# Attention scores of two chunks at a time, with four masks in 32-row tiles and eight PSUM banks

## The chip, the cores and the metric

The kernel runs on one core of one Trainium2 chip. The core has TensorE (matmuls; its weight loads are shown apart as PEld), VectorE (DVE), ScalarE (ACT), GpSimd (POOL) and SyncE (SP, which issues nearly all DMAs here). Matmul results go to PSUM, eight banks of 128 partitions by 512 float32. Everything else lies in SBUF, here one buffer called `arena`. The metric is the device time of one execution in microseconds (us).

## The reference

Routed attention, then an MLP mixer:

```python
q_assign = argmax(einsum('bhsd,hcd->bhsc', q_n, c_n), -1)   # 16 clusters per head
k_assign = argmax(einsum('bhsd,hcd->bhsc', k_n, c_n), -1)
mask   = q_assign[:, :, :, None] == k_assign[:, :, None, :]
scores = where(mask, q @ k.T / sqrt(64), -1e9)
attn   = softmax(scores);  x = attn @ v                     # B 4, H 8, S 768, D 64
h = relu(x.transpose(0, 2, 1) @ w_tok1) @ w_tok2            # 768 -> 256 -> 768
u = x + h.transpose(0, 2, 1)
out = u + relu(u @ w_ch1) @ w_ch2                           # 512 -> 1536 -> 512
```

All is float32. The change touches the attention alone.

## The kernel before, in words

The 32 heads are worked off as 16 pairs (`pair(m)`). In a pair head 0 has partitions 0 to 63 and head 1 partitions 64 to 127 of the transposed q and k, `Ts[m % 3]`, so that the two heads of one step go to TensorE as two row tiles of 64 rows, at positions (0, 0) and (64, 0), with results in two PSUM banks.

`scores(m)` works in twelve chunks: six blocks of 128 keys (`i`) by two halves of 384 queries (`u`). For each chunk and head there is one float32 matmul of 64 rows (`plain`; each float32 matmul becomes two instructions on TensorE), and onto the same bank one bf16 matmul, the mask: key one-hots times query one-hots of the clusters, scaled so that pairs of different clusters get about -2**33. The one-hots are in `Ms[m % 2]`, rows 64h to 64h + 16; the rows up to the tile's end are zero. After that ScalarE takes the exp of both banks (L1205) into the `exs` buffers. Three pairs of banks are used in turn (`s = n % 3`, banks 0 to 5); banks 6 and 7 belong to the values. Pair 0 is built a little otherwise: its first three chunks' scores run ahead of the masks.

After the scores come the values (`values`, L1238): for each of the six key blocks sixteen matmuls in 128 by 32 tiles, four side by side, added up in banks 6 and 7. After the first of them stand the sums of the pair before (`sums(m - 1, 5)`), which are softmax denominators: a matmul of ones with `es`, the exps added up by DVE. `add_up` makes two half sums `es[0]` and `es[1]` with four additions of 128x1536; where `FOLD[m]` is "V", DVE adds these two together as well and `sums` needs one group of matmuls, where it is "-" it needs two. Before the fifth block stands `route(m + 2, 0)`: four matmuls with the centroids into bank 0, on DVE a transpose (L1098), a maximum (L1099), a comparison and a transpose (L1103), on ScalarE a scaling to bf16 (L1108). That result goes to DRAM (`wdm`) and back into `Ms` with two DMAs, one for each head. `finish_x` has DVE transpose the values out of banks 6 and 7 (L1285), transpose the sums (L1293), and, every second pair, divide.

ScalarE also splits q and k of a later pair into 16-bit halves for a DMA transpose (`part_qk`) and joins the halves (`join_qk`), both at L875, eight copies in a pair. DVE meanwhile rounds the mixer's weights piece by piece and stores combinations of them for later.

The order of the work is fixed in the program. TensorE runs in the order of the code. For the other engines a planner (`Program.plan`) simulates the kernel with costs written in the code (`COST`, the numbers at `mm`, `SWITCH = 0.1` where a matmul's tile shape, `mode`, differs from that of the one before) and picks at each time the ready operation with the earliest due time. On the chip each engine keeps that order, and semaphores do the waiting.

After the attention come token mixing and channel mixing, in which TensorE works with 128 by 128 tiles and DVE and POOL combine operands and results. These parts are not edited, but their order on DVE, ACT, POOL and SP comes from the same plan.

Of the kernel before, what the change touches and what calls it, by code (L numbers as in the profile page):

```python
# [19 lines left out]
C = 16  # L20
P = 128
NJ = S // P
# [7 lines left out]
HJ = NJ // 2  # L30
HS = HJ * P
# [18 lines left out]
GRAIN = 32  # L50
BUSY, HITS_AT = 12, 18.0
CHECK_AT = 532.0
FOLD = "-VVVVVVVVVV-----"

COST = {
    "ACT": (0.09, 0.00083),
# [667 lines left out]
def kernel(  # L724
# [26 lines left out]
    nc = tc.nc  # L751
    g = Program()
# [9 lines left out]
    wdm = [dram.tile([P, HS], BF16, name=f"wdm{i}") for i in range(2)]  # L762
# [77 lines left out]
    def bank(*i):  # L840
        return [("ps", n) for n in i]


    def mm(dst, lhsT, rhs, start, stop, cost, rd, wr, pos=None, tr=None):
        def fn(e):
            nc.tensor.matmul(  # L846
                dst, lhsT=lhsT, rhs=rhs, start=start, stop=stop, tile_position=pos,
                is_transpose=tr, skip_group_check=True,
            )

        return g.add({"PE": cost}, fn, rd, wr, mode=(lhsT.shape[0], lhsT.shape[1]))

    def turn(dst, src, rd, wr, start=True, stop=True):
        return mm(
# [46 lines left out]
    def dma(dst, src, rd, wr, kb, row, after=0.0, queue="SP"):  # L901

        q = {"SP": nc.sync, "ACT": nc.scalar, "POOL": nc.gpsimd}[queue]
        return g.add(
            {queue: ISSUE}, lambda e: q.dma_start(dst, src), rd, wr, (kb * 1024, row), after  # L905
        )
# [172 lines left out]
    def route(m, bk):  # L1079

        T, M, hp = Ts[m % 3], Ms[m % 2], m % (H // 2)
        for gr in range(4):
            r0 = (NJ + HJ * gr) % NQK
            mm(
                ps[32 * gr : 32 * gr + 32, bk, 0:HS], cbd.ap[:, hp],
                T.ap[:, r0 : r0 + HJ].rearrange("p a t -> p (a t)"), True, True, 0.161,
                T.rows(r0, r0 + HJ) + cbd.k(), bank(bk), pos=(0, 32 * gr),
            )  # L1090
        a, e, o = rt[0:3]
        if m == 0:
            o = o0

        def blocks(t):
            return t.ap.rearrange("p (n c) -> p n c", c=C)

        vec(lambda: nc.vector.transpose(out=a.ap, in_=ps[:, bk, 0:HS]), 0.57, bank(bk), a.k())  # L1098
        vec(lambda: nc.vector.reduce_max(out=mxs.ap[:, 0:24], in_=blocks(a), axis=AX.X), 0.54,  # L1099
            a.k(), mxs.k())  # L1100
        tt(blocks(e), blocks(a), mxs.ap[:, 0:24].unsqueeze(2).to_broadcast([P, 24, C]),
           ALU.is_ge, HS, a.k() + mxs.k(), e.k())
        vec(lambda: nc.vector.transpose(out=o.ap, in_=e.ap), 0.56, e.k(), o.k())  # L1103

        r = rb if m else rb0
        g.add(
            {"ACT": 0.75},
            lambda e: nc.scalar.activation(  # L1108
                out=r.ap, in_=o.ap, func=ACT.Identity, scale=msc.ap[:, 0:1],
                bias=msc.ap[:, 1:2], accum_out=hits.ap[:, m : m + 1],  # L1110
            ),
            o.k() + msc.k(), r.k() + [("hits", m)], after=0.0 if m else HITS_AT,
        )

        if m == 0:
            for gr in (0, 2, 3, 1):
                i, u = divmod(gr, 2)
                for h in range(2):
                    rows = slice(32 * gr, 32 * gr + 32)
                    dst = M0.ap[64 * h : 64 * h + 32, i, u * HS : (u + 1) * HS]  # L1120

                    def place0(e, dst=dst, rows=rows, i=i, h=h):
                        sc = [msc0.ap[rows, n, h : h + 1] for n in range(2)]
                        if e == "ACT" and i:
                            nc.scalar.activation(
                                out=dst, in_=o.ap[rows], func=ACT.Identity, scale=sc[0], bias=sc[1]
                            )
                        elif e == "ACT":
                            nc.scalar.copy(out=dst, in_=o.ap[rows])  # L1129
                        elif i:  # L1130
                            nc.vector.tensor_scalar(
                                out=dst, in0=o.ap[rows], scalar1=sc[0], scalar2=sc[1],
                                op0=ALU.mult, op1=ALU.add,
                            )
                        else:
                            nc.vector.tensor_copy(out=dst, in_=o.ap[rows])

                    g.add(
                        {"ACT": (0.5, 0.65)[i], "DVE": (0.35, 0.45)[i]}, place0,
                        o.k() + msc0.k() + M0.k(), [("mask", 0, i, u, h)],  # L1140
                    )
            for Mn in Ms:
                vec(
                    lambda Mn=Mn: nc.vector.memset(Mn.ap, 0.0), 0.7,
                    [("mask", 0, 1, u, h) for u in range(2) for h in range(2)], Mn.k(),
                )
            return
        dma(wdm[m % 2], rb.ap, rb.k(), [("wdm", m % 2)], 96, 768)
        for h in range(2):
            dma(  # L1150
                M.ap[64 * h : 64 * h + C].rearrange("c i (u n) -> c (i u) n", u=2),
                wdm[m % 2].rearrange("(g r) n -> r g n", g=4)[C * h : C * h + C],
                [("wdm", m % 2)] + M.k(),
                [("mask", m % 2, i, u, h) for i in range(2) for u in range(2)], 48, 768,
            )


    nex = 0
# [2 lines left out]
    def scores(m):  # L1161
        nonlocal nex
        T, M = Ts[m % 3], Ms[m % 2] if m else M0
        st = unit[m] = [exs[(nex + i) % len(exs)] for i in range(NJ)]
        nex += NJ

        def chunk(n):
            return divmod(n, NJ) if m == 0 else divmod(n, 2)[::-1]

        def plain(n):  # L1170
            u, i = chunk(n)
            s, r0 = n % 3, NJ + HJ * u
            for h in range(2):
                hs = slice(64 * h, 64 * h + 64)
                mm(
                    ps[:, 2 * s + h, 0:HS], T.ap[hs, i],
                    T.ap[hs, r0 : r0 + HJ].rearrange("p a t -> p (a t)"), True, False, 0.3225,
                    T.rows(i, i + 1) + T.rows(r0, r0 + HJ), bank(2 * s + h), pos=(64 * h, 0),
                )

        ahead = 3 if m == 0 else 0
        for n in range(ahead):
            plain(n)
        if m == 0:
            turn_qk(1, (7, 6, 7))
            load_qkr(3, 18.0)
        for n in range(2 * NJ):
            u, i = chunk(n)
            s = n % 3
            if n >= ahead:  # L1190
                plain(n)
            for h in range(2):
                hs = slice(64 * h, 64 * h + 64)
                mm(
                    ps[:, 2 * s + h, 0:HS], M.ap[hs, 1, i * P : (i + 1) * P],
                    M.ap[hs, 0, u * HS : (u + 1) * HS], False, True, 0.081,
                    [("mask", m % 2, a, c, h) for a, c in ((1, i // HJ), (0, u))] + M.k(),
                    bank(2 * s + h), pos=(64 * h, 0),
                )
            if m == 0 and n == ahead - 1:  # L1200
                route(1, 6)
            ex = st[i]
            g.add(
                {"ACT": 0.70},
                lambda e, ex=ex, s=s, u=u: nc.scalar.activation(  # L1205
                    out=ex.ap[:, :, u * HS : (u + 1) * HS], in_=ps[:, 2 * s : 2 * s + 2, 0:HS],
                    func=ACT.Exp, scale=SM_SCALE,
                ),
                bank(2 * s, 2 * s + 1),
                ex.rows(0, 2, u * HS, (u + 1) * HS) + ([("exps", m)] if n == 2 * NJ - 1 else []),  # L1210
            )

    def add_up(m):
        st = unit[m]
# [113 lines left out]
    def pair(m):  # L1328
        scores(m)
        if m >= 1 and m + 2 < NP:  # L1330
            join_qk(m + 2)
        if m:
            next_qk(m)
        for i in range(NJ):
            if i == 3 and m == 0:
                turn_qk(2, (1, 2, 3))
            if i == 4 and 1 <= m < NP - 2:
                route(m + 2, 0)
            if i == 1:
                if m:  # L1340
                    sums(m - 1, 5)
                    finish_x(m - 1, 5, 1)
                add_up(m)
            values(m, i)
        if m == NP - 1:
            sums(m, 4)
        finish_x(m, 5, 0)
        if m == NP - 1:
            finish_x(m, 4, 1)
        if m == 0:  # L1350
            load_v(2)
            route(2, 5)
            next_qk(m)
        if m + 3 < NP:
            load_v(m + 3)
# [620 lines left out]
    for m in range(NP):  # L1976
        pair(m)
# [78 lines left out]
```

## Time and profile before

| | |
|---|---|
| median of 3 runs | 789.91 us (789.84 to 790.67) |
| profiled execution | 789.87 us, its span 788.0 us |
| TensorE busy | 777.8 us, 99% of the span |
| DVE, ACT, POOL busy | 675.2, 461.4, 194.1 us |
| chain that ended last | 95% TensorE |
| granted TensorE clock | 0.999 |
| one pair in steady state | 19.3 us, attention until about 335 us |

The busy shares say how full an engine is over the whole span. The chain of work that ended last is followed back from the last instruction, at each step to what released it. In time order it tells how long TensorE spends on each step of a pair. A matmul row of the trace is longer than the time for which the next one has to wait, because matmuls are pipelined; starts are compared, not lengths. In brackets stands the engine's idle time before a row, and what ended it.

### The profile page before, as it was taken

To read this page: it belongs to the slowest core of one execution; us is meant where nothing else is said; L and a number is where in the kernel's file an instruction comes from. 1 tells how busy PE (TensorE), PEld (TensorE's weight loads), DVE (VectorE), ACT (ScalarE), POOL (GpSimd) and SP (SyncE) were. 2 spreads that over 40 slices of the span, in tenths; PEclk is the share of its full clock that TensorE was granted. 3 is DMA by queue.
4 is the path that set the end of the run, shared out by engine and by line. 5 is a ranking of instruction groups with operands and counts; after the bars stand their busy time and mean duration, and the time that the engine had idled before them with its cause. 6 is when DMAs were issued, how large, how long until landed. Compare 5 with 4: busy or idle time off the path is not lost.

```text
span 788.0 us, 15324 instructions
## 1 busy us (share of the span) xinstructions
PE 777.8 (99%) x5975; PEld 463.1 (59%) x5975; DVE 675.2 (86%) x848; ACT 461.4 (59%) x614; POOL 194.1 (25%) x187
## 2 busy tenths in 40 slices
PE   8999999999999999999999999999999999999996
PEld 5666666666666666545555555555555555555554
DVE  6979999999998999999999877999853576799964
ACT  5788888889889875599614368633235204400422
POOL 0000000000000000001274598700285289830000
PEclk9999999999999999999999999999999999999999
DMA  9676668876778953568848999975788744444666
GB/s 249 169 192 180 170 154 221 212 202 178 196 196 215 266 178 128 127 135 202 195 124 253 313 281 266 273 189 132 168 189 177 165 100 101 105 105 102 160 164 161
DMA packets 326576, 143.68 MB, mean 182 GB/s; under 512 B 260192, under 2 KB 322400, under 8 KB 326496
## 3 DMA queue, kind: packets, MB, share of 16 engines
q1 hardware_dynamic: 324128, 141.83, 71.6%
q8 instruction: 49, 0.80, 0.4%
q10 hardware_dynamic: 2368, 0.79, 0.4%
q14 instruction: 31, 0.25, 0.1%
HBM read 91.95 MB, written 28.61 MB: 153 GB/s over the span
## 4 chain that ended last, share of the span: by engine, by line
PE 95%; DVE 3%; DMA 1%; issue 0%; ACT 0%; SPq 0%
PE ps L846 77%; PE ps L1238 18%; DVE arena L885 2%; DMA arena<-in_q_dram 1%; DMA arena<-in_moe_w_ch_dram 0%; ACT arena L865 0%; DVE arena L1384 0%; DVE arena L1390 0%; DVE arena L1387 0%; SPq L905 0%; DVE arena L1380 0%; DVE arena L867 0%; ACT arena L1129 0%
## 5 line engine op out<-in xcount | busy, mean ns | idle before, releaser
L846 PE MATMUL ps<-arena 128*128 128x384 f32 (+5 forms) x2727 | 640.2, 463 | 4.5 <-POOL arena masks.py:199 1.4
L846 PEld LDWEIGHTS ps<-arena 128*128 128x128 f32 (+2 forms) x2343 | 340.1, 184 | 250.3 <-issue 61.6
L885 DVE TENSOR_TENSOR arena<-arena 128x1536 f32<-128x1536 f32 (+6 forms) x340 | 369.9, 1109 | 12.5 <-issue 3.6
L885 POOL TENSOR_TENSOR arena<-arena 128x384 f32<-128x384 f32 x181 | 193.4, 1109 | 501.8 <-DVE arena L885 378.6
L885 DVE TENSOR_TENSOR arena<-ps,arena 128x384 f32<-128x384 f32 (+3 forms) x227 | 189.4, 844 | 78.4 <-PE ps L846 76.0
L875 ACT COPY arena<-arena 128x768 uint16<-128x768 uint16 x221 | 189.2, 955 | 62.6 <-DMA arena<-arena 32.8
L1205 ACT ACTIVATE arena<-ps 128x768 f32<-128x768 f32 x192 | 150.7, 811 | 35.2 <-PE ps L846 33.4
L1238 PE MATMUL ps<-arena 128*32 128x192 f32 (+1 forms) x3248 | 144.9, 335 | 0.0
L1238 PEld LDWEIGHTS ps<-arena 128*32 128x32 f32 x3248 | 103.7, 110 | 44.1 <-issue 15.6
L865 ACT COPY arena<-ps 128x512 f32<-128x512 f32 (+2 forms) x44 | 31.3, 719 | 116.1 <-PE ps L846 114.8
L892 ACT ACTIVATE arena<-arena 128x1152 f32<-128x1152 f32 (+1 forms) x38 | 39.7, 1070 | 51.0 <-DVE arena L885 50.3
L1912 ACT ACTIVATE arena<-arena 128x768 f32<-128x768 f32 x40 | 38.7, 969 | 32.8 <-DMA arena<-in_moe_w_ch_dram 27.1
L846 PEld LDWEIGHTS <-arena 64*128 64x128 bf16 x384 | 19.2, 94 | 24.6 <-issue 0.2
L1390 DVE SCALAR_TENSOR_TENSOR arena<-arena 128x512 f32<-128x512 uint32 (+1 forms) x31 | 21.5, 713 | 0.4
L1384 DVE SCALAR_TENSOR_TENSOR arena<-arena 128x512 uint32<-128x512 uint32 (+1 forms) x31 | 20.9, 695 | 0.3
L1108 ACT ACTIVATE arena<-arena 128x384 bf16<-128x384 f32 x16 | 11.2, 701 | 13.6 <-issue 13.6
L1380 DVE TENSOR_SCALAR arena<-arena 128x512 uint32<-128x512 uint32 (+1 forms) x31 | 13.9, 458 | 4.0 <-DMA arena<-in_moe_w_tok_dram 4.0
L1285 DVE STREAM_TRANSPOSE arena<-ps 128x768 f32<-128x768 f32 x16 | 15.2, 952 | 0.4 <-PE ps L1238 0.4
L1387 DVE TENSOR_SCALAR arena<-arena 128x512 uint32<-128x512 uint32 (+1 forms) x31 | 12.8, 436 | 0.4
L1293 DVE STREAM_TRANSPOSE arena<-ps 128x384 f32<-128x384 f32 x16 | 9.3, 579 | 2.2 <-PE ps L1238 2.0
L1098 DVE STREAM_TRANSPOSE arena<-ps 128x384 f32<-128x384 f32 x16 | 9.1, 571 | 1.8 <-PE ps L846 1.8
L1103 DVE STREAM_TRANSPOSE arena<-arena 128x384 f32<-128x384 f32 x16 | 9.3, 578 | 0.6
(57 smaller groups left out, 47.2 us busy)
## 6 DMA issues: line engine op xcount, KB each, us to landing
arena<-wd SPq DMA_DIRECT2D x196, 192.0 KB, 3.0
wd<-arena SPq DMA_DIRECT2D x84, 224.0 KB, 3.0
arena<-in_moe_w_ch_dram SPq DMA_DIRECT2D x96, 128.0 KB, 3.1
arena<-in_moe_w_ch_dram SPq DMA_DIRECT2D x16, 768.0 KB, 5.3
arena<-in_v_dram SPq DMA_DIRECT2D x16, 384.0 KB, 4.8
out_dram<-arena SPq DMA_DIRECT2D x14, 384.0 KB, 3.5
arena<-in_k_dram SPq DMA_DIRECT2D x13, 384.0 KB, 4.2
arena<-in_q_dram SPq DMA_DIRECT2D x13, 384.0 KB, 4.2
```

Of the source, the lines that this page charges most:

```text
L846: nc.tensor.matmul(dst, lhsT=lhsT, rhs=rhs, start=start, stop=stop, tile_position=pos, is_transpose=tr, skip_group_check=True,)
L865: nc.scalar.copy(out=dst, in_=src)
L875: nc.scalar.copy(out=dst, in_=src)
L885: (nc.vector if e == "DVE" else nc.gpsimd).tensor_tensor(out=dst, in0=a, in1=b, op=op)
L892: nc.scalar.activation(out=dst, in_=src, func=ACT.Relu)
L1205: lambda e, ex=ex, s=s, u=u: nc.scalar.activation(out=ex.ap[:, :, u * HS : (u + 1) * HS], in_=ps[:, 2 * s : 2 * s + 2, 0:HS], func=ACT.Exp ...
L1238: nc.tensor.matmul(dst, lhsT=lhsT, rhs=rhs, start=start, stop=stop, tile_position=pos, skip_group_check=True,)
L1285: lambda: nc.vector.transpose(out=x.ap[:, :, cols].rearrange("p j (c d) -> p c j d", d=32), in_=ps[:, 6:8, 0:HS],),
L1380: vec(lambda: nc.vector.tensor_scalar(out=hh, in0=hi, scalar1=0x07FFFFFF, scalar2=3, op0=ALU.bitwise_and, op1=ALU.logical_shift_left,), f, ...
L1384: vec(lambda: nc.vector.scalar_tensor_tensor(out=TT, in0=hi, scalar=0xC0000000, in1=hh, op0=ALU.bitwise_and, op1=ALU.bitwise_or), 0.14 + 0 ...
L1390: vec(lambda: nc.vector.scalar_tensor_tensor(out=ll, in0=lo, scalar=float(2.0**-52), in1=hh.bitcast(F32), op0=ALU.mult, op1=ALU.mult,), 0. ...
L1912: lambda e, i=i, func=func, bias=bias, n=n, hi=hi: nc.scalar.activation(out=hi, in_=hi, func=func, bias=bias, accum_out=wsum.ap[:, i, n : ...
```

## The change

In the pairs 1 to 15 `scores` goes by two chunks: the four float32 matmuls of both, then their four masks, then their two exps. A mask is now a matmul of 32 rows. The one-hots are stored twice for each head, in rows 64h and 64h + 32, so that the first half of the queries (`u` = 0) uses one 32-row tile and the second half the other. The two chunks of one group are the two halves for one key block, so its four masks sit at row positions 0, 32, 64 and 96, in four banks. Loading `Ms` takes four DMAs instead of two. The planner is told `mode=(64, P)` for these masks, the same as for the scores, and half their former cost.

Chunks go round over four pairs of banks, banks 6 and 7 among them, in the order 0, 1, 2, 3, 0, 1, 2, 3, 0, 1, 3, 2. The sums of the pair before move from after the first value to before it, and from bank 5 to bank 1. `FOLD` has "V" for pairs 1 to 8, before for 1 to 10. Pair 0 computes as before.

```diff
-FOLD = "-VVVVVVVVVV-----"
+FOLD = "-VVVVVVVV-------"
...
-        return g.add({"PE": cost}, fn, rd, wr, mode=(lhsT.shape[0], lhsT.shape[1]))
+        return g.add({"PE": cost}, fn, rd, wr, mode=mode or (lhsT.shape[0], lhsT.shape[1]))
...
         for h in range(2):
-            dma(
-                M.ap[64 * h : 64 * h + C].rearrange("c i (u n) -> c (i u) n", u=2),
-                wdm[m % 2].rearrange("(g r) n -> r g n", g=4)[C * h : C * h + C],
-                [("wdm", m % 2)] + M.k(),
-                [("mask", m % 2, i, u, h) for i in range(2) for u in range(2)], 48, 768,
-            )
+            for dup in range(2):
+                r0 = 64 * h + 32 * dup
+                dma(
+                    M.ap[r0 : r0 + C].rearrange("c i (u n) -> c (i u) n", u=2),
+                    wdm[m % 2].rearrange("(g r) n -> r g n", g=4)[C * h : C * h + C],
+                    [("wdm", m % 2)] + M.k(), [("mask", m % 2, h, dup)], 48, 768,
+                )
...
+        def slot(n):
+            return n % 3 if m == 0 else (0, 1, 2, 3, 0, 1, 2, 3, 0, 1, 3, 2)[n]
...
+        def masks(n):
+            u, i = chunk(n)
+            s = slot(n)
             for h in range(2):
-                hs = slice(64 * h, 64 * h + 64)
+                r0, r1 = (64 * h, 64 * h + 64) if m == 0 else (64 * h + 32 * u, 64 * h + 32 * u + 32)
...
                 mm(
-                    ps[:, 2 * s + h, 0:HS], M.ap[hs, 1, i * P : (i + 1) * P],
-                    M.ap[hs, 0, u * HS : (u + 1) * HS], False, True, 0.081,
-                    [("mask", m % 2, a, c, h) for a, c in ((1, i // HJ), (0, u))] + M.k(),
-                    bank(2 * s + h), pos=(64 * h, 0),
-                )
+                    ps[:, 2 * s + h, 0:HS], M.ap[r0:r1, 1, i * P : (i + 1) * P],
+                    M.ap[r0:r1, 0, u * HS : (u + 1) * HS], False, True, 0.081 if m == 0 else 0.0405,
+                    key + M.k(), bank(2 * s + h), pos=(r0, 0), mode=(64, P),
+                )
...
+        if m:
+            for n in range(0, 2 * NJ, 2):
+                for fn in (plain, masks, exps):
+                    fn(n)
+                    fn(n + 1)
+            return
...
         for i in range(NJ):
+            if i == 0 and m:
+                sums(m - 1, 1)
+                finish_x(m - 1, 1, 1)
...
             if i == 1:
-                if m:
-                    sums(m - 1, 5)
-                    finish_x(m - 1, 5, 1)
                 add_up(m)
```

More of the change, by code (lines that the diff above doesn't have):

```diff
@@ L841, in bank, with mm @@
         return [("ps", n) for n in i]
-    def mm(dst, lhsT, rhs, start, stop, cost, rd, wr, pos=None, tr=None):
+    def mm(dst, lhsT, rhs, start, stop, cost, rd, wr, pos=None, tr=None, mode=None):
         def fn(e):
@@ L1168, in chunk @@
             return divmod(n, NJ) if m == 0 else divmod(n, 2)[::-1]
+        def slot(n):
+            return n % 3 if m == 0 else (0, 1, 2, 3, 0, 1, 2, 3, 0, 1, 3, 2)[n]
         def plain(n):
             u, i = chunk(n)
-            s, r0 = n % 3, NJ + HJ * u
+            s, r0 = slot(n), NJ + HJ * u
             for h in range(2):
@@ L1179, in plain, with exps @@
                 )
[L1181 to L1187, printed above, removed]
+        def masks(n):
             u, i = chunk(n)
-            s = n % 3
-            if n >= ahead:
-                plain(n)
+            s = slot(n)
             for h in range(2):
-                hs = slice(64 * h, 64 * h + 64)
-                mm(
-                    ps[:, 2 * s + h, 0:HS], M.ap[hs, 1, i * P : (i + 1) * P],
-                    M.ap[hs, 0, u * HS : (u + 1) * HS], False, True, 0.081,
-                    [("mask", m % 2, a, c, h) for a, c in ((1, i // HJ), (0, u))] + M.k(),
-                    bank(2 * s + h), pos=(64 * h, 0),
-                )
-            if m == 0 and n == ahead - 1:
-                route(1, 6)
-            ex = st[i]
+                r0, r1 = (64 * h, 64 * h + 64) if m == 0 else (64 * h + 32 * u, 64 * h + 32 * u + 32)
+                key = (
+                    [("mask", 0, a, c, h) for a, c in ((1, i // HJ), (0, u))] if m == 0
+                    else [("mask", m % 2, h, u)]
+                )
+                mm(
+                    ps[:, 2 * s + h, 0:HS], M.ap[r0:r1, 1, i * P : (i + 1) * P],
+                    M.ap[r0:r1, 0, u * HS : (u + 1) * HS], False, True, 0.081 if m == 0 else 0.0405,
+                    key + M.k(), bank(2 * s + h), pos=(r0, 0), mode=(64, P),
+                )
+        def exps(n):
+            u, i = chunk(n)
+            s, ex = slot(n), st[i]
             g.add(
                 {"ACT": 0.70},
-                lambda e, ex=ex, s=s, u=u: nc.scalar.activation(
+                lambda e: nc.scalar.activation(
                     out=ex.ap[:, :, u * HS : (u + 1) * HS], in_=ps[:, 2 * s : 2 * s + 2, 0:HS],
@@ L1211, in scores @@
             )
+        if m:
[4 more added lines that the diff above has]
+            return
+        ahead = 3
+        for n in range(ahead):
+            plain(n)
+        turn_qk(1, (7, 6, 7))
+        load_qkr(3, 18.0)
+        for n in range(2 * NJ):
+            if n >= ahead:
+                plain(n)
+            masks(n)
+            if n == ahead - 1:
+                route(1, 6)
+            exps(n)
     def add_up(m):
```

## Prediction, before the changed kernel was run

> **What bounds the kernel now.** I read the page first (busy shares, the chain that ended last), then the chain in order of time over the attention stage, then the weight loads and ScalarE inside one pair of heads.
>
> ```profile
> span 788.0 us, 15324 instructions
> PE 777.8 (99%) x5975; PEld 463.1 (59%) x5975; DVE 675.2 (86%) x848; ACT 461.4 (59%) x614; POOL 194.1 (25%) x187
> PE 95%; DVE 3%; DMA 1%; issue 0%; ACT 0%; SPq 0%
> ```
>
> TensorE is busy 99% of the span and holds 95% of the chain. So what counts is TensorE time, and the waits that a changed order puts on TensorE. The chain shows one pair of heads like this (start, length, line, matmul instructions):
>
> ```profile
> 168.62 10.08 PE ps L846 x72
> 178.70 5.98 PE ps L1238 x136
> 184.69 0.65 PE ps L846 x8
> 185.33 2.60 PE ps L1238 x64
> 187.93 9.89 PE ps L846 x72
> ...
> 255.57 6.63 PE ps L1238 x144
> ```
>
> One pair takes 19.31 us (168.62 to 187.93): scores with masks (72 instructions), sums of the pair before and four values (136), the route (8), two values (64). Two values take 2.60, so one takes 1.30. The row with 144 instructions is a pair whose sums are not folded: eight more instructions cost 0.65. The route shows the same: 8 instructions are two passes of 384 float32 columns in four column tiles side by side, so one pass is 0.325. Of fifteen such score stages eight take 10.08 or 10.09 and seven 9.89. Inside one stage the weight loads give the parts:
>
> ```profile
> 168.55 0.30 PEld L846 LDWEIGHTS ps<-arena 64*128 64x128 f32 x4 [0.30 <-DVE arena L1099]
> 168.98 0.10 PEld L846 LDWEIGHTS <-arena 64*128 64x128 bf16 x2
> 169.30 0.36 PEld L846 LDWEIGHTS ps<-arena 64*128 64x128 f32 x4 [0.22 <-issue]
> 169.78 0.10 PEld L846 LDWEIGHTS <-arena 64*128 64x128 bf16 x2
> ...
> 176.57 0.36 PEld L846 LDWEIGHTS ps<-arena 64*128 64x128 f32 x4 [0.22 <-issue]
> ...
> 177.62 0.30 PEld L846 LDWEIGHTS ps<-arena 64*128 64x128 f32 x4 [0.47 <-ACT arena L1205]
> ```
>
> Masks start together with the float32 loads of the next chunk (169.30 to 176.57 is nine chunks, 0.808 each), and the bf16 loads of the next masks start with its second pass. So 169.30 to 169.78 is two masks and one pass: 0.48 less 0.32 leaves 0.16 for two masks side by side. A chunk is 0.65 of scores and 0.16 of masks; twelve are 9.69, and 9.89 leaves 0.20 for the entry from the values' tiles. The last row is the 0.20 by which eight stages are longer: TensorE waits for an exp to free its banks. ScalarE shows why:
>
> ```profile
> 169.67 6.52 ACT L1205 ACTIVATE arena<-ps 128x768 f32<-128x768 f32 x8 [2.67 <-PE ps L846]
> 176.09 0.70 ACT L1108 ACTIVATE arena<-arena 128x384 bf16<-128x384 f32 x1
> 176.68 0.19 ACT L1108 ACTIVATION_READ_ACCUMULATOR arena<-arena 128x1 f32 x1
> 176.78 2.90 ACT L1205 ACTIVATE arena<-ps 128x768 f32<-128x768 f32 x4
> 179.54 6.79 ACT L875 COPY arena<-arena 128x768 uint16<-128x768 uint16 x8
> ```
>
> Eight exps come at TensorE's pace (0.81), then the route's activation takes 0.70, and the next four run at ScalarE's own pace: 2.90 for four, of which one lasts 0.81, so 0.70 from start to start.
>
> **The change, part by part.**
>
> Masks in 32-row tiles. Per pair twelve groups of two masks (0.16 each) become six groups of four. If four run at once, one group is 0.16, and 0.01 for two more issues. Per pair 0.90 is saved, if nothing else moves.
>
> The price is that TensorE now goes from 64-row tiles to 32-row tiles and back in each group. Before, scores and masks had the same tiles: the mask loads above stand 0.32 ahead of their use, under the running pass, and nothing is lost. No row of before goes from 64 to 32 rows. The nearest are two changes of row tile alone, at the start of the kernel (windows cut to a few instructions; PE is the matmul, PEld the load that follows):
>
> ```profile
> 11.53 0.74 PE L846 MATMUL ps<-arena 64*128 64x384 f32 x2
> 11.94 0.14 PEld L846 LDWEIGHTS ps<-arena 128*128 128x128 f32 x1 [0.54 <-issue]
> ...
> 13.65 0.54 PE L846 MATMUL ps<-arena 128*128 128x128 f32 x3
> 13.85 0.11 PEld L846 LDWEIGHTS <-arena 64*128 64x128 bf16 x4 [0.17 <-issue]
> 13.86 0.50 PE L846 MATMUL ps<-arena 64*128 64x384 bf16 x4
> ```
>
> The pass begun at 11.53 has streamed its columns by 11.85; the next load, in 128-row tiles, starts at 11.94, and no wait ends there. The transpose begun at 13.65 (128 columns, 0.11) is through at 13.76, and the first 64-row load comes at 13.85. Each time 0.09 us pass in which no weights load. After it the bf16 weights cost next to nothing: four such matmuls from 13.86 end at 14.36, so the second two began 0.17 after the first two. The float32 entry above costs 0.20: 0.09 idle, and 0.11 for weights that can't be loaded ahead. So I take 0.10 for going to 32 rows and 0.20 for coming back. The ends are 0 for both (the row without a change of tile), and 0.20 for both.
>
> One group is then 1.29 of scores, 0.17 of masks, 0.10 in and 0.20 back: 1.76 against 1.61. Six groups are 10.56, with the entry from the values among the returns, against 9.89. That is +0.67 a pair, and over pairs 1 to 15 +10.1 us.
>
> The Trainium skill, in "TensorEngine Tiling (Array Packing)", section Key Properties, says that changing the tiling mode, not only the tile, drains TensorE, and its list of modes has 64×128 and 32×128 apart. By that rule the drain is paid and the sum stands; by the trace's row of 64-row matmuls after 64-row matmuls, read as "row tiles mix freely", it would be rival 1. The trace agrees as far as it goes (0.09 between 64 and 128 rows); no run here shows 64 to 32.
>
> Eight banks. Scores now rotate over four pairs of banks, not three, so one late exp no longer stops TensorE: the 0.20 of eight stages goes, -1.6 us. The fourth pair, banks 6 and 7, is the values' own, so two waits are new. First, chunk 3 of a pair needs DVE's transpose of the values before it. In the listing of the new order only one 1536-wide addition stands between the route's transpose and this one:
>
> ```profile
> L885 DVE TENSOR_TENSOR arena<-arena 128x1536 f32<-128x1536 f32 x98 | 170.4, 1748 | 6.1 <-PE ps L1238 2.1 <-ACT arena L1205 1.1
> 208.16 0.94 DVE L1285 STREAM_TRANSPOSE arena<-ps 128x768 f32<-128x768 f32 x1
> ```
>
> Even with a whole addition (1.75) begun just before, it ends 2.7 after the values, while TensorE has 0.20 + 1.29 + 0.47 + 0.65 = 2.6 of other work: nothing, or 0.1. Second, the values need the exp of chunk 10, which uses banks 6 and 7. The first exp above starts 0.37 after its masks and lasts 0.81; add 0.05 for the release, and TensorE may go on 1.22 after the last masks started. Until then it has masks (0.16), the switch (5.98 - 4×1.30 - 0.65 = 0.13) and the sums, now put here (0.65): 0.94. So 0.28 is waited in the pairs with folded sums, eight now: +2.2. Unfolded sums are 1.30 and cover it.
>
> The last exp of a pair now stands behind four joining copies (listing of ScalarE's order). 6.79 for eight is 3.4 for four; the exp ends some 5.4 after the last masks, and the values need it at 0.94 + 0.28 + 5×1.30 + 0.65 = 8.4. Free; without that cover it would cost up to the 3.4.
>
> Sums earlier: the same work in another place, counted above. They need additions that DVE ends in the score stage, as before.
>
> FOLD: two pairs more with unfolded sums, 2×0.65 = +1.3 on TensorE, and 2×1.75 = 3.5 us less on DVE. DVE is the second engine:
>
> ```profile
> 149.30:168.60 19.30, 19.30 (x283) 12.01 (x282) 18.64 (x24) 16.54 (x22) 0.00 (x0) 1.00 0.64 169
> 384.00:410.00 26.00, 25.02 (x76) 13.67 (x74) 25.64 (x42) 7.01 (x7) 13.95 (x13) 1.00 0.69 171
> ```
>
> (columns: window, length, then busy of PE, PEld, DVE, ACT, POOL). It works 18.6 of 19.3 in a pair, and at 384 to 410 TensorE idles 1.0 behind it. With DVE relieved by 3.5 and TensorE later by ten, I take that 1.0 as gone.
>
> Mask DMAs: four loads instead of two, 30 issues more on SyncE.
>
> ```profile
> 180.90 0.87 SPq L905 DMA_DIRECT2D arena<-wdm  x2
> DMA to landing us min/median/max: 1.6/2.5/5.4
> ```
>
> Two issues take 0.87; with two more the masks of the pair at 187.93 would be on their way by 182.7 and, at the median, land by 185.2, some 4 us before their first use at 187.93 + 1.3. Loads queued behind move 0.9. Free; a landing at the maximum of 5.4 would still make it, by 1 us.
>
> Sum: +10.1 - 1.6 + 2.2 + 1.3 - 1.0 = +11.0. The profiled execution took 789.87 (span 788.0 and 1.9 around it), within 0.04 of the median of the runs, 789.91. Forecast 800.9. With the price of the return between 0.09 and 0.20 (75 added returns, up to -8.3) and the way in up to 0.20 (90, up to +9) this case reaches from 793 to 810.
>
> **The rivals.**
>
> 1. No drain between 64 and 32 rows: both are row tiles, and loads run ahead as before. For it speaks that the row tiles of 64 already run side by side and load ahead; against it the two gaps of 0.09. Place: 90 groups. A group is 1.46, six and the entry 8.96, -0.93 a pair, -14.0. Now ScalarE is the tighter: 1.40 for two exps and once 0.70 for the route between them, so the exp of chunk 10 is some 0.6 later, and eight pairs wait 0.9 (+7), the other seven about 0.2 (+1.5). -14.0 - 1.6 + 8.5 + 1.3 = -5.8: 784.1, 779 to 788. DVE bounds it, since it has 0.7 of idle time in a pair and 3.5 of folds taken off. The point that decides: the other terms sum to -13, over some 82 round trips, so below 0.16 us for in and back together the change gains.
>
> 2. The four tiles don't run at once but two and two, so the change doesn't do what it says. Two row tiles at once are shown, and four column tiles (the route), four row tiles nowhere. 0.16 in 90 groups: +14.4, 815 with the drain. Without the drain 1. becomes about 791, with no wait at chunk 10 beyond my 0.28.
>
> The Trainium skill, in "TensorE: Matmul & The Clock Gate", Part 3, gives 3.07 and not 4 as the measured gain of four 32-row tiles. By that figure a group of masks would be 0.21, an estimate, and the sum 805; no run here shows it.
>
> **How the numbers follow.** My sum (drain paid, four at once): 0.52. Rival 1: 0.29. Rival 2 with drain 0.09, without 0.05. The last 0.05 is something that I have not seen, either way. What a measurement can tell from no change is about 0.2%, 1.6 us. Slower 0.64, same 0.05 (rival 2 without drain reaches into it), faster 0.31. The range must take in rival 1: 782 to 808 holds nearly all of my case, three quarters of rival 1 and the 791. My case alone: 793 to 810.
>
> **What would show it.** A score stage in the chain of 10.5 to 10.6 (right) or 9.0 (rival 1); 32-row bf16 loads that follow the end of the scores by 0.09 instead of standing under them; then 0.20 to the next float32 pass. The group of four masks 0.17 long or 0.33 (rival 2). A wait for the exps (L1206 there) of 0.3 between sums and values in pairs 2 to 9, none in the middle of the scores. No idle TensorE from 395 to 420. Wrong: 32-row loads that start under 64-row passes.

## The result, and the profile after

| | median of runs | ratio to before, 95% interval |
|---|---|---|
| before | 789.88 us (789.12 to 790.67) | |
| changed | 803.82 us (803.74 to 803.97) | 1.0177 [1.0159, 1.0194] |

The changed kernel is 13.9 us slower; 800.9 was forecast. The page says the same of the engines as before: TensorE 99% busy, now of a longer span.

```profile
span 802.0 us, 15368 instructions
PE 790.7 (99%) x5991; PEld 453.3 (57%) x5991; DVE 669.2 (83%) x848; ACT 455.8 (57%) x614; POOL 190.3 (24%) x185
PE 93%; DVE 3%; ACT 2%; issue 1%; POOL 0%; DVEq 0%; POOLq 0%
```

The chain of the changed kernel in order of time (start, length, line, instructions), over a pair with folded sums, the first two rows of a pair without, and the start of the last pair's values:

```profile
174.38 10.64 PE ps L846 x72
185.06 0.82 ACT arena L1206
185.92 5.41 PE ps L1258 x128
191.33 0.65 PE ps L846 x8
191.97 2.60 PE ps L1258 x64
...
235.23 10.59 PE ps L846 x72
245.82 6.63 PE ps L1258 x144
...
327.01 9.74 PE ps L1258 x213
```

The score stage takes 10.59, before 10.09 or 9.89. Where the chain says 10.64 it leaves TensorE for an exp (L1206), and the row runs on to the end of the last matmul. By the starts it is the same there within 0.01: the stage's first load begins at 174.31 (below) and the first load of the sums, which come next, at 184.89.

```profile
184.89 0.16 PEld L1258 LDWEIGHTS ps<-arena 128*32 128x32 f32 x8 [0.17 <-issue]
185.92 0.16 PEld L1258 LDWEIGHTS ps<-arena 128*32 128x32 f32 x8 [0.87 <-ACT arena L1206]
```

The second row is the first load of the values, which waits for the exp. From 174.38 to the route at 191.33 it is 16.95. Less the 10.59, and the 5.98 that the same sums and values took before, that leaves 0.38 of waiting. Without folded sums 6.63 is unchanged.

The last pair's values start 12.8 later than before, where the chain has

```profile
314.21 10.52 PE ps L1238 x224
```

From there to the end of the span it is 475.0, before 473.8.

The weight loads of one group show what the trip to the 32-row tiles costs (in brackets idle time of the load engine, and what ended it):

```profile
174.31 0.95 PEld L846 LDWEIGHTS ps<-arena 64*128 64x128 f32 x8 [0.30 <-issue]
175.80 0.10 PEld L846 LDWEIGHTS <-arena 32*128 32x128 bf16 x4 [0.55 <-issue]
176.07 0.95 PEld L846 LDWEIGHTS ps<-arena 64*128 64x128 f32 x8 [0.17 <-issue]
177.56 0.10 PEld L846 LDWEIGHTS <-arena 32*128 32x128 bf16 x4 [0.55 <-issue]
```

Before, the bf16 loads stood 0.32 ahead of their matmuls, under the last pass of the scores. Here they come after the scores have streamed through: a group's pace is 177.56 - 175.80 = 1.76, of which 1.29 is scores. From the bf16 loads to the next float32 loads it is 0.27, made of four masks and the change back: with 0.16 for the masks, as for two before, 0.1 is left in which nothing loads or streams. That four masks take no longer than two is shown below, in the kernel with one chunk in a group.

ScalarE has time to spare between groups now:

```profile
176.18 1.51 ACT L1206 ACTIVATE arena<-ps 128x768 f32<-128x768 f32 x2 [2.44 <-PE ps L846]
177.94 1.51 ACT L1206 ACTIVATE arena<-ps 128x768 f32<-128x768 f32 x2 [0.25 <-PE ps L846]
```

Two exps end 0.25 before the next two may start. In the list of waits over the attention (engine and line, released by: total, times, longest) DVE has a wait that before came to 1.1 us in 4 times:

```profile
DVE arena L885 <- ACT arena L1206: 20.7, 19, 5.9
```

It waits, in its fixed order, for exps that come later than its order was made for. In the windows of both kernels (window, length, then busy of PE, PEld, DVE, ACT, POOL) this is seen best. The token stage's windows differ in length; each holds TensorE's last wait of that stage. Before, attention and then token stage:

```profile
33.00:325.00 292.00, 292.00 (x4245) 182.33 (x4242) 273.81 (x353) 237.33 (x312) 0.00 (x0) 1.00 0.73 192
325.00:424.00 99.00, 97.94 (x269) 49.91 (x268) 96.03 (x152) 65.63 (x81) 28.68 (x27) 1.00 0.70 167
```

Changed:

```profile
33.00:337.00 304.00, 302.66 (x4252) 171.52 (x4254) 267.55 (x349) 231.24 (x312) 0.00 (x0) 1.00 0.70 187
337.00:430.00 93.00, 91.50 (x255) 46.01 (x248) 89.27 (x146) 62.79 (x79) 24.86 (x23) 1.00 0.70 160
```

The attention is 12 us longer, but DVE does 6 us less in it (267.55 against 273.81; 3.5 of this are the two additions left out), and idles 36 us there instead of 18. TensorE idles 1.5 us in the token stage, before 1.1.

### The profile page after: what moved, and what is told of

It is laid out like the page before. It is cut to its first block, busy times and chain, and to the rows that moved or that the text cites. A ratio compares the mean times of both kernels' runs of the same rounds, so it can differ in the third digit from the quotient of the medians.

```text
span 802.0 us, 15368 instructions
## 1 busy us (share of the span) xinstructions
PE 790.7 (99%) x5991; PEld 453.3 (57%) x5991; DVE 669.2 (83%) x848; ACT 455.8 (57%) x614; POOL 190.3 (24%) x185
## 4 chain that ended last, share of the span: by engine, by line
PE 93%; DVE 3%; ACT 2%; issue 1%; POOL 0%; DVEq 0%; POOLq 0%
PE ps L846 76%; PE ps L1258 17%; DVE arena L885 2%; ACT arena L875 1%; ACT arena L1206 1%; ACT arena L865 1%; DVE arena L1404 0%; DVE arena L1407 0%; DVE arena L1410 0%; DVE arena L1400 0%; DVE arena L867 0%; ACT arena L1129 0%; POOL arena masks.py:199 0%; POOL arena masks.py:197 0%; DVEq L885 0%
## 5 line engine op out<-in xcount | busy, mean ns | idle before, releaser
L846 PE MATMUL ps<-arena 128*128 128x384 f32 (+6 forms) x2727 | 650.1, 469 | 4.3 <-DVE arena L885 1.7
L885 DVE TENSOR_TENSOR arena<-arena 128x1536 f32<-128x1536 f32 (+6 forms) x340 | 365.8, 1097 | 28.3 <-ACT arena L1206 20.7
L885 POOL TENSOR_TENSOR arena<-arena 128x384 f32<-128x384 f32 x179 | 189.6, 1092 | 519.6 <-DVE arena L885 393.8
L885 DVE TENSOR_TENSOR arena<-ps,arena 128x384 f32<-128x384 f32 (+3 forms) x227 | 189.6, 845 | 79.5 <-PE ps L846 75.5
L1206 ACT ACTIVATE arena<-ps 128x768 f32<-128x768 f32 x192 | 146.5, 809 | 64.5 <-PE ps L846 64.2
L1258 PE MATMUL ps<-arena 128*32 128x192 f32 (+1 forms) x3264 | 147.9, 336 | 1.3 <-ACT arena L1206 1.2
L846 PEld LDWEIGHTS <-arena 32*128 32x128 bf16 (+1 forms) x384 | 10.2, 91 | 50.4 <-issue 49.2
```

The costliest lines, as they stand in the source:

```text
L846: nc.tensor.matmul(dst, lhsT=lhsT, rhs=rhs, start=start, stop=stop, tile_position=pos, is_transpose=tr, skip_group_check=True,)
L885: (nc.vector if e == "DVE" else nc.gpsimd).tensor_tensor(out=dst, in0=a, in1=b, op=op)
L1206: lambda e: nc.scalar.activation(out=ex.ap[:, :, u * HS : (u + 1) * HS], in_=ps[:, 2 * s : 2 * s + 2, 0:HS], func=ACT.Exp, scale=SM_SCALE,),
L1258: nc.tensor.matmul(dst, lhsT=lhsT, rhs=rhs, start=start, stop=stop, tile_position=pos, skip_group_check=True,)
```

## The experiments

Each compares with the kernel before on the same chip; what is cut or moved is shown against the changed kernel, where nothing else is said.

**Masks in 64-row tiles again** (e1_masks64). The one-hots are loaded once, and the planner's cost of a mask goes back to 0.081, both as before the change. All else of the change stays.

```diff
-            for dup in range(2):
...
+            dma(M.ap[64 * h : 64 * h + C]..., [("mask", m % 2, h, dup) for dup in range(2)], 48, 768)
...
-                r0, r1 = (64 * h, 64 * h + 64) if m == 0 else (64 * h + 32 * u, 64 * h + 32 * u + 32)
+                r0, r1 = 64 * h, 64 * h + 64
```

> The changed kernel with its masks as 64-row tiles again, two at a time, and their one-hots loaded once; groups of two chunks, eight banks, early sums and eight folds stay. Theory (each group pays 0.10 for going to 32-row tiles and 0.20 for coming back): no gap in a group, a score stage of 9.9 us instead of 10.6, 15 x 0.72 = 10.8 us less than the changed kernel's 803.8: about 793, and still 3 above the kernel before, for the wait of the values on the exp of chunk 10 and the two unfolded sums. Rival (the groups of two chunks, the eight banks or the doubled mask loads cost it): 800 or more, score stages above 10.3.

Measured 791.80 us, 1.0028 [1.0017, 1.0039] of before. The chain has

```profile
187.82 9.89 PE ps L846 x72
197.71 0.78 PE ps L1256 x8
198.49 0.02 issue
198.51 5.41 PE ps L1256 x128
...
207.16 9.89 PE ps L846 x72
217.05 6.63 PE ps L1256 x144
```

and the loads of a group

```profile
169.80 0.10 PEld L846 LDWEIGHTS <-arena 64*128 64x128 bf16 x2 [0.22 <-issue]
169.97 1.00 PEld L846 LDWEIGHTS ps<-arena 64*128 64x128 f32 x8
```

Float32 loads follow bf16 loads without a gap, and every score stage is 9.89. The 32-row tiles, together with the doubled loads that they need, are worth 12 us, of which the score stages make 15 × 0.70 = 10.5. Groups of two chunks and eight banks cost none of that. This run doesn't part the tiles from the loads, but in the changed kernel's list of waits over the attention no load and no matmul of TensorE waits for a DMA.

What is left, 2.2 us over before, has two parts. The last values start 1.0 later than before: the two unfolded sums (1.3) and eight short waits of the values (0.78 + 0.02 + 5.41 against 5.98, 1.8 in all), less the eight waits that the banks removed (1.6) and 0.5 of an earlier start. The rest lies behind: from 325 to 424 TensorE idles 2.5 us, before 1.1. This run's order on DVE was made for the pace that TensorE has, DVE's additions wait only 1.4 us for exps in the attention, and eight pairs are folded as in the changed kernel. So a fitting order and less work for DVE aren't all that the idle time in the token stage hangs on; what else does is not shown.

**One chunk in a group** (e2_one_chunk), which doubles the trips to 32-row tiles. The planner's cost of a mask goes back to 0.081.

```diff
-            for n in range(0, 2 * NJ, 2):
-                for fn in (plain, masks, exps):
-                    fn(n)
-                    fn(n + 1)
+            for n in range(2 * NJ):
+                for fn in (plain, masks, exps):
+                    fn(n)
```

> The changed kernel with one chunk in a group: twelve trips to 32-row tiles in a pair instead of six, two masks each. Theory: a chunk is 0.645 + 0.16 + 0.10 + 0.20 = 1.11, a score stage 13.3 instead of 10.6, +40 us over 15 pairs; the exp of chunk 10 then ends in time, -2: about 841. Rival (no price for the trip; the four masks of a group are slow because they write four banks at once): two masks in 0.16 and nothing else, a stage of 9.9 and 793.

A single execution took 842.11 us.

```profile
168.97 13.35 PE ps L846 x72
182.32 5.98 PE ps L1257 x136
```

```profile
169.75 0.10 PEld L846 LDWEIGHTS <-arena 32*128 32x128 bf16 x2 [0.55 <-issue]
170.01 0.30 PEld L846 LDWEIGHTS ps<-arena 64*128 64x128 f32 x4 [0.17 <-issue]
```

From the bf16 loads of two masks to the next float32 loads it is 0.26. In the changed kernel it is 0.27 for four, so four masks do take the time of two.

Six trips more made the stage 13.35 - 10.59 = 2.76 longer. Of this 6 × 0.16 = 0.96 is that two masks now take the time of four; the rest, 1.80, is 0.30 a trip, as in the sum. The wait between scores and values is gone as well, as chunk 10's masks end a chunk earlier.

**The planner told** (e3_true_plan). No instruction is added or removed, only the order on DVE, ScalarE, POOL and SyncE changes.

```diff
-SWITCH = 0.1
+SWITCH = 0.15
...
-                    key + M.k(), bank(2 * s + h), pos=(r0, 0), mode=(64, P),
+                    key + M.k(), bank(2 * s + h), pos=(r0, 0), mode=(64 if m == 0 else 32, P),
```

> The changed kernel, its planner told that the masks' tiles differ from the scores' (0.15 for each change of tiles), so that the order on DVE and ScalarE is made for TensorE's true pace; no instruction more or less. Theory: DVE's idle time in the attention, where it waits in order for late exps, goes down from 36 us, more rounding of weights is done there, and TensorE's idle time of 1.6 us between 338 and 424 shrinks: 802 to 803. Rival (those waits have nothing to do with the order): 803.8 and the same idle time.

Measured 801.39 us, 1.0147 [1.0132, 1.0163], 2.4 below the changed kernel's median, more than expected; the two intervals of the ratio touch. The windows tell where:

```profile
33.00:337.00 304.00, 302.58 (x4252) 171.51 (x4252) 285.47 (x385) 232.89 (x312) 0.00 (x0) 1.00 0.76 204
337.00:430.00 93.00, 92.44 (x260) 47.19 (x253) 84.33 (x134) 65.11 (x86) 23.02 (x23) 1.00 0.69 158
```

The attention is as long as in the changed kernel, but DVE does 285.47 us of work in it instead of 267.55: its additions (L885) wait 2.0 us there for exps instead of 20.7. The last values start at 327.02, and from there to the end of the span it is 472.6, 2.4 less than in the changed kernel and 1.2 less than before. TensorE idles 0.56 in the token stage instead of 1.5. The rest of the 2.4 can't be read off step by step; the load engine's idle time that DVE ended, from 335 on, is 9.5 us instead of 12.8.

**The kernel before with four pairs of banks** (e4_four_slots), and nothing else of the change (diff against before).

```diff
+        def slot(n):
+            return n % 3 if m == 0 else (0, 1, 2, 3, 0, 1, 2, 3, 0, 1, 2, 0)[n]
...
-            s, r0 = n % 3, NJ + HJ * u
+            s, r0 = slot(n), NJ + HJ * u
...
-            s = n % 3
+            s = slot(n)
```

> The kernel before, with nothing changed but the banks: chunks go over four pairs of banks in the order 0 1 2 3 0 1 2 3 0 1 2 0, so that banks 6 and 7 are given back after chunk 7. Theory: the eight waits of 0.20 for an exp vanish, every score stage is 9.9, and the values wait for nothing new: -1.6, about 788.3. Rival (chunk 3 waits for the transpose of the values before it on DVE, or the new order costs elsewhere): 789.9 or more.

Measured 788.35 us, 0.9979 [0.9962, 0.9995].

```profile
167.10 9.89 PE ps L846 x72
176.99 5.98 PE ps L1241 x136
...
186.22 9.97 PE ps L846 x72
```

The stages of 10.09 are gone. One stage of fifteen, the 9.97, has 0.08 left: there the loads of chunk 3 wait for DVE's transpose of the values. This version is the fastest so far, 0.2% faster than the kernel before.

**Banks 6 and 7 given back early in the changed kernel** (e5_values_free).

```diff
-            return n % 3 if m == 0 else (0, 1, 2, 3, 0, 1, 2, 3, 0, 1, 3, 2)[n]
+            return n % 3 if m == 0 else (0, 1, 2, 3, 0, 1, 2, 3, 0, 1, 2, 0)[n]
...
-                sums(m - 1, 1)
-                finish_x(m - 1, 1, 1)
+                sums(m - 1, 3)
+                finish_x(m - 1, 3, 1)
```

> The changed kernel with the bank order 0 1 2 3 0 1 2 3 0 1 2 0 and the early sums in bank 3 instead of 1: banks 6 and 7 are given back after chunk 7, so the values wait for no late exp. Theory: the 0.29 between the masks' end, the sums and the values goes in the eight pairs with folded sums, -2.3: about 801.5, sums and four values together 5.98 again. Rival (that stretch is longer for another reason, the sums' own place or their bank): 803.8 and no change there. What the plan makes of it moves both by about 1.

Measured 807.91 us, 1.0211 [1.0151, 1.0272]: a miss of 6. The interval is wide and holds the changed kernel's 1.0177, so the traces must tell.

```profile
195.06 8.88 PE ps L846 x60
203.94 0.80 ACT arena L1206
204.78 1.19 PE ps L846 x8
205.97 5.98 PE ps L1258 x136
```

Sums and values take 5.98 again, so the reason given for the wait holds. But the wait has only moved: chunk 11 now needs the banks of chunk 8, one group before it, and waits there. From 195.06 to 211.95 it is 16.89, before the edit 16.95 (174.38 to 191.33). In the seven pairs without folded sums, which waited for nothing, the same wait is new. The last values start at 330.30, 3.3 later than in the changed kernel, of a span that is 4.5 longer. In groups of two, three chunks are too short a way round; in e4_four_slots, a chunk at a time, they were enough.

**Ten folds in the changed kernel** (e6_fold10), as before the change.

```diff
-FOLD = "-VVVVVVVV-------"
+FOLD = "-VVVVVVVVVV-----"
```

> The changed kernel with ten pairs folded, as before. Theory: two more pairs save 0.65 of sums and pay the wait of 0.29, -0.7 on TensorE; 3.5 us more on DVE, which idles 36 us in the attention, so part of it is free and part is waited for in the token stage: 803 to 804.5. Rival (unfolding two pairs was a real loss of 1.3): 802.5 or less.

Measured 808.62 us, 1.0215 [1.0156, 1.0274], more than either expected. The intervals of this and of the changed kernel overlap, so the traces must tell.

```profile
33.00:337.00 304.00, 302.31 (x4241) 170.77 (x4237) 267.12 (x341) 230.79 (x312) 0.00 (x0) 1.00 0.68 181
337.00:430.00 93.00, 89.59 (x238) 45.07 (x239) 88.86 (x146) 61.25 (x77) 22.77 (x21) 0.98 0.73 174
```

In the chain the last score stage starts at 315.88, in the changed kernel at 316.43: the 0.5 is gained. After it TensorE idles 3.4 us from 337 to 430, instead of 1.5. DVE does no more in the attention than with eight folds, so the two additions have pushed other work into the token stage. That explains a part only: the span is 5.3 longer than the changed kernel's. The granted clock was 0.83 from 420 to 430, 1.00 in that stretch of the changed kernel, and what that cost isn't parted from the rest.

**Sums after the first value** in the changed kernel (e7_sums_late); bank 1 stays.

```diff
-            if i == 0 and m:
-                sums(m - 1, 1)
-                finish_x(m - 1, 1, 1)
...
             if i == 1:
+                if m:
+                    sums(m - 1, 1)
+                    finish_x(m - 1, 1, 1)
                 add_up(m)
```

> The changed kernel with the sums after the first value again (bank 1 stays). Theory: the values then wait 0.93 for the exp of chunk 10 with nothing in between, in all fifteen pairs; eight pairs lose the 0.65 that the sums covered, seven lose 0.93: +11.7, about 815. Rival (the values don't wait for that exp, the sums' place is worth nothing): 803.8.

A single execution took 816.70 us.

```profile
179.84 10.64 PE ps L846 x72
...
190.53 0.82 ACT arena L1206
...
191.39 6.05 PE ps L1258 x136
```

Nothing of TensorE lies between scores and values, and the values wait 0.91 (190.48 to 191.39) for the exp of chunk 10, in pairs with folded sums and without. The last values start 12.9 us later than in the changed kernel, as much as the whole time differs. So much are the early sums worth here: without them the wait that banks 6 and 7 bring stands bare in every pair.

**Ten folds with the planner told** (e8_true_fold10): the edits of e3_true_plan and e6_fold10 together.

> The changed kernel with ten pairs folded and the planner told of the change of tiles: e3_true_plan and e6_fold10 together. Theory (e6_fold10 lost 5 in the token stage because its order on DVE was made for a TensorE that is faster than the real one, so that DVE idled in the attention and was late afterwards): the two folds' 3.5 us fit into the attention, and the 0.5 that e6_fold10 gained there stays: 800.5 to 802. Rival (DVE has no room for two more folds, whatever the order): 804 or more, and TensorE idle for over 3 us in the token stage.

Measured 801.64 us, 1.0145 [1.0130, 1.0161].

```profile
33.00:337.00 304.00, 302.25 (x4243) 171.10 (x4240) 287.43 (x381) 233.08 (x312) 0.00 (x0) 1.00 0.75 201
337.00:430.00 93.00, 92.22 (x258) 46.57 (x251) 86.19 (x139) 65.02 (x85) 24.11 (x23) 1.00 0.71 168
```

DVE has room for two more folds once its order fits TensorE's pace: 287.43 us of work in the attention, 0.8 us of idle TensorE in the token stage. The fold is then worth nothing that can be measured against e3_true_plan (801.39).

**Four pairs of banks, and 0.15 for a change of tiles in the planner** (e9_slots_plan: the kernel of e4_four_slots with `SWITCH = 0.15`).

> e4_four_slots with 0.15 instead of 0.1 in the planner for a change of tiles (the trace has 0.13 and 0.20). Theory: the order was already made for nearly the right pace, two changes in a pair make 0.1 us, so 788 to 789 as in e4_four_slots. Rival (the order for the true pace is worth 1 us here too): 787.4 or less.

Measured 788.29 us, 0.9978 [0.9969, 0.9987]: the same as e4_four_slots. Here, where the planner's pace was nearly right, nothing is to be had from it.

## Why the prediction was right, point by point

- *The price of the tiles* (0.10 in, 0.20 back; +10.1 with the masks' saving). Right. The stage is 10.59, the sum said 10.56. Putting the masks back into 64-row tiles took 12 us off, doubling the trips gave 0.30 for each. Rival 1, no drain, falls: bf16 loads never start under the scores. The row that the price came from, a change between 64 and 128 rows, was near enough.
- *Four masks at once*. Right: from the bf16 loads to the next float32 loads it is 0.27 with four masks and 0.26 with two. Rival 2 falls. The 805 that the prediction took, as an estimate, from the 3.07 of the Trainium skill ("TensorE: Matmul & The Clock Gate", Part 3) isn't borne out either: it has four masks 0.05 longer than two.
- *Eight banks*, -1.6 and +2.2. The first is shown alone in e4_four_slots (788.35 against 789.64). The second had place and cause right, as e5_values_free and e7_sums_late show, and its size too small: 0.38 in eight pairs, 3.0, where 0.28 and 2.2 were taken. That chunk 3 pays nothing for the transpose held: no stage of the changed kernel is longer for it.
- *Unfolded sums*, +1.3. Right as a price on TensorE: 6.63 against 5.98 before, in two pairs more.
- *The last exp behind four copies, four mask loads*: free, as taken: in the changed kernel's list of waits TensorE's loads wait for no masks, and for a copy on ScalarE three times, 0.2 at most.
- *"I take that 1.0 as gone"* is the step that failed. From the last values to the end the changed kernel takes 1.2 more than before, not 1.0 less, and TensorE idles 1.5 in the token stage; from 395 to 420, where no idle time was to be, it idles 0.5. The reason given, DVE with 3.5 us less to do and TensorE ten later, left out in what order DVE works. Its order was made for a TensorE that changes tiles for nothing; on the chip DVE waited for late exps and did the rounding of weights afterwards. With the planner told, DVE's waits for exps fell from 20.7 to 2.0, and the same stretch takes 1.2 less than before: then the term is about right. A fitting order alone doesn't assure it, as the 2.5 of idle time in e1_masks64 show, where TensorE is later by only 1.0.

By the rows, the span's 14.0 are 12.8 up to the start of the last values and 1.2 behind it. The 12.8 are, within 0.1, fifteen stages of 10.59 against eight of 10.09 and seven of 9.89 (+8.9), the waits (+3.0) and the sums (+1.3), less a start 0.3 earlier. The forecast was 2.9 us too low: about 2.2 of that is the term behind the last values and 0.8 the wait. The stages' 0.4 and the earlier start cancel.

## What to carry to other kernels

Before matmuls are packed into smaller row tiles, count the changes of tile size that the packing brings: here a trip to 32-row tiles and back cost 0.30 us, more than the 0.16 that four masks at once save. By these figures, as an estimate that no run tests, one trip would have had to serve some four chunks to pay. A row for another pair of tile sizes in the same trace was a sound price here. Where the order of the other engines comes from a plan, a wrong cost on one engine can be paid a second time on the others: here it was 2.4 us.

## What was not expected of the hardware

The forecast gave its own sum a chance of only 0.52, and two things were open. The change between 64 and 32 rows costs about what the changes of tile shape measured before cost, 0.09 to 0.1 us without any load or stream, although both are row tiles of the same width. And four 32-row tiles that write four banks run in the time of two (0.27 against 0.26 up to the next loads), about 0.16 for 384 columns in bf16.
